# The last four bias steps placed inside the first two attention steps

## The chip, the cores and the metric

The kernel runs on one core of a Trainium2 chip. The metric is the device time of one execution in microseconds; lower is better. The core's engines take their own instructions in order: PE (matrix products), DVE, ACT and POOL (elementwise work), and SP, which here only issues DMA. "bias write" below is the ACT instruction that reads a bias step's product from PSUM.

## The reference

Attention with a learned relative-position bias, then a dense two-layer block on the attention output:

```python
scores = scale * np.matmul(q, k.transpose(0, 1, 3, 2))       # B 4, H 8, S 576, D 64
psi_rel = np.log1p(np.abs(rel))                              # rel = i - j
psi_i = np.log1p(np.maximum(pos[:, None], 1.0))
x = (psi_rel / psi_i)[..., None]
h = np.maximum(x @ w1 + b1, 0.0)                             # 32 hidden units
bias = h @ w2                                                # one value per head
scores = scores + bias.transpose(2, 0, 1)[None]
attn = np.exp(scores - max); attn = attn / (sum + 1e-09)
x = (attn @ v) as (2304, 512)
h = x @ w_in; r = np.maximum(h, 0.0); g = s * (r * r) + b    # w_in 512 x 2048
return g @ w_out
```

A constant added to one row of scores leaves the result as it is, since the row is normalised.

## The kernel before, in words

**Bias stage.** The 576 query rows are made in 36 steps of 16 rows (`STEPS`). A step has four *features* of 128 x 576 elements (4 query rows x 32 hidden units on the partitions), one for each `c` in 0 to 3. `feature` (L114 to L126) puts each on an engine by a letter: `v` is DVE (L121), `p` is POOL (L123), `a` is ACT (L125). The letters are "vvpa", "vppa", "vpvp" for steps 0, 1, 2 modulo 3; the last four steps have letters of their own (`ends`, L112). The features come from a pool of 16 buffers. `bias_step` (L131 to L154) multiplies the four features with the second layer's weights on PE (L140, L143) into a PSUM tile of two banks, writes the tile to SBUF on ACT (L147, tile `stg`), and lets SP store it to DRAM (L153, `bias`). From step 24 on `first_head` (L156 to L165) also copies head 0's rows straight into the tiles that the first pair reads: `bt` for rows below 512 (two DMAs a step), `be` for the last 64 rows (steps 32 to 35, two DMAs each). The stores of the last four steps are kept back until step 35.

PSUM has three pools here: `ps_s` (two tiles of two banks, scores), `ps_x` (one tile of two banks, the attention output) and `ps_t` (two banks, turns). Steps 2 modulo 3 use `ps_x`, the others `ps_s`.

**Attention stage.** There are 16 pairs (a head, two batches) of five blocks of 128 query rows: 80 blocks. `step(n)` (L525 to L561) runs in a software pipeline: `probs_t(n)` turns block n's exponentials on PE (L299) and copies them to the tile `pt` (ACT L330, DVE L332); `scores(n + 2)` makes the products on PE (L236) into `ps_s`; `biased` adds the bias on DVE (L250); `expo` takes the exponential on ACT (L261); and, from pair 1 on, `av` (L366, L369) makes the output of the pair before. In step 1 `probs_t` also takes the `ps_x` tile for a spare turn (L310). `split_qk` (L207 to L213) splits q or k of a pair into a high and a low part with two POOL instructions (L211, L212); scores need both. `load_w` fetches raw weight blocks and `fill` decodes them in pieces within the steps from pair 1 on, beginning with an ACT instruction (L407).

**Order.** The order is written out by hand: within each engine the instructions follow the order of the program. The loop at L599 makes the features of step `st + 2`, then runs step `st`, then what `plan` (L586 to L598) lists for `st`. So `scores(0)` stands behind step 33, `scores(1)` behind step 35, and `step(0)` behind the loop.

**Matrix stage.** From 286 us on, the two dense layers run (`expand`, L476; `project`, L501), with sums in 18 tiles `acc` of 128 x 512 in a pool of their own (L650).

Of the kernel before, what the change touches and what calls it, by code (L numbers as in the profile page):

```python
# [9 lines left out]
F32 = mybir.dt.float32  # L10
# [16 lines left out]
def attention_moe(ctx, tc, q, k, v, w_in, w_out, dist, par, out):  # L27
    nc = tc.nc
    NB, H, S, D = 2 * q.shape[0], q.shape[1], k.shape[3] - 64, q.shape[2] // 2
    DM, DFF = w_out.shape[1], w_out.shape[0]  # L30
    NT = out.shape[0]
# [4 lines left out]
    STEPS = S // 16  # L36
# [5 lines left out]
    LAST = 5 * NP  # L42
# [12 lines left out]
    ps_t = ps_ctx.enter_context(tc.tile_pool(name="ps_t", bufs=2, space=PSUM))  # L55
    pss_ctx = ExitStack()
    ps_s = pss_ctx.enter_context(tc.tile_pool(name="ps_s", bufs=2, space=PSUM, side="right"))
    dctx = ExitStack()
    dp = dctx.enter_context(tc.tile_pool(name="dp", bufs=1, side="right"))
    fp = dctx.enter_context(tc.tile_pool(name="fp", bufs=16, side="right"))  # L60
# [48 lines left out]
        nc.vector.tensor_copy(sb, pt_[:, 2:4])  # L109

    feats, late = {}, []
    ends = {STEPS - 4: "vvvp", STEPS - 3: "vvva", STEPS - 2: "vpva", STEPS - 1: "vpva"}  # L112

    def feature(st, c):  # L114
        w = NU - S - 16 * st - 4 * c
        f = fp.tile([128, S // 64, 68], F32, tag="f", name="f")[:, :, 0:64]
        src = ls[:, w:w + S].rearrange("p (a b) -> p a b", b=64)
        col = slice(4 * st + c, 4 * st + c + 1)
        kind = (ends.get(st) or ("vvpa", "vppa", "vpvp")[st % 3])[c]
        if kind == "v":  # L120
            nc.vector.tensor_scalar(f, src, thr[:, col], None, op0=ALU.max)  # L121
        elif kind == "p":
            nc.gpsimd.tensor_scalar(f, src, FLT_MAX, thr[:, col], op0=ALU.min, op1=ALU.max)  # L123
        else:
            nc.scalar.activation(f, src, AF.Relu, bias=off[:, col])  # L125
        return f, kind == "a"  # L126

    def bias_features(st):
        feats[st] = [feature(st, c) for c in (2, 0, 3, 1)]

    def bias_step(st):  # L131
        f2, f0, f3, f1 = feats.pop(st)
        fs = (f0, f1, f2, f3)
        if st % 3 == 2:
            ps = ps_x.tile([128, 2, 512], F32, tag="x", name="bps")
        else:
            ps = ps_s.tile([128, 2, 512], F32, tag="s", name="bps")
        pb = ps.rearrange("p a b -> p (a b)")
        for c in range(4):
            nc.tensor.matmul(  # L140
                pb[32 * c:32 * c + 32, 0:512], w2bd, fs[c][0][:, 0:8], start=True, stop=True)
        for c in range(4):
            nc.tensor.matmul(  # L143
                pb[32 * c:32 * c + 32, 512:S], w2bd, fs[c][0][:, 8:9], start=True, stop=True)
        kcol = kc[:, 1:2] if fs[3][1] else kc[:, 0:1]
        stg = fp.tile([128, S], F32, tag="stg", name="stg", bufs=10)
        nc.scalar.activation(stg, pb[:, 0:S], AF.Identity, scale=nr[:, st:st + 1], bias=kcol)  # L147
        if st >= 24:
            first_head(st, stg)
        late.append((st, stg))  # L150
        if st < STEPS - 4 or st == STEPS - 1:
            for i, t in late:
                nc.sync.dma_start(out=bias_d[:, 16 * i:16 * i + 16, :].rearrange("h r j -> r h j"), in_=t)  # L153
            late.clear()  # L154
# [16 lines left out]


    qs, ks, vals, tts, bts, pts, units, accs = {}, {}, {}, {}, {}, {}, {}, {}
    sums, rows, rts, rbs, bes, xts = {}, {}, {}, {}, {}, {}

    def load_bias(p, t0, t1):
        h = pairs[p][0]
# [111 lines left out]
    def probs_t(n):  # L289
        p, t = divmod(n, 5)  # L290
        if p not in pts:
            pts[p] = (ptp.tile([128, 4, 2, S], F32, tag="pt", name="pt"),
                      ptp.tile([128, S], F32, tag="ptr", name="ptr"))
        pt, ptr = pts[p]
        halves = [slice(64 * r, 64 * r + 64) for r in range(2)]

        def turn(outs, src, start=True):
            for r, d in enumerate(halves):
                nc.tensor.matmul(outs[r], src[d], ident[d, d], is_transpose=True,  # L299
                                 start=start, stop=True, skip_group_check=not start)  # L300

        def tail_of(t):
            return units[5 * p + t][0].rearrange("p x j -> p (x j)")[:, 512:640]

        def spare(j):
            c = HALF + 64 * j
            return [accs[p - 1][:, r, c:c + 64] for r in range(2)]

        if p == 0 and t == 1:
            accs[-1] = ps_x.tile([128, 2, 512], F32, tag="x", name="xps")  # L310
        if t == 3:
            nc.scalar.activation(
                ptr[:, 0:384].rearrange("p (t r c) -> p t r c", t=3, r=2),
                accs[p - 1][:, :, HALF:HALF + 192].rearrange("p r (t c) -> p t r c", t=3), AF.Copy)
        if (n + 1, 1) in tts:
            expo(n + 1, 1)
        pr = units[n][0]
        pss = [ps_t.tile([128, 512], F32, tag="t", name="tps") for _ in range(2)]
        if t < 4:
            for i in range(8):  # L320
                kb, x = divmod(i, 2)
                k0 = 64 * x + 128 * kb
                turn([ps[:, 64 * i:64 * i + 64] for ps in pss], pr[:, x, k0:k0 + 128])
            for j in ((), (0, 1), (2,), ())[t]:
                turn(spare(j), tail_of(j), start=(p == 0))
            for r, d in enumerate(halves):
                o = pt[:, :, :, 128 * t + 64 * r:128 * t + 64 * r + 64]
                i = pss[r].rearrange("p (a x b) -> p a x b", a=4, x=2)
                if r == 0:
                    nc.scalar.activation(o, i, AF.Copy)  # L330
                else:
                    nc.vector.tensor_copy(o, i)  # L332
            return
        for i in range(4):
            turn([ps[:, 64 * i:64 * i + 64] for ps in pss], pr[:, 0, 128 * i:128 * i + 128])
        turn([ps[:, 384:448] for ps in pss], tail_of(3))
        turn([ps[0:64, 256:320] for ps in pss], pr[:, 0, 512:S])
        turn([ps[0:9, 320:384] for ps in pss], rows.pop(p))
        rts[p] = sm.tile([9, 128], F32, tag="rt", name="rt", bufs=1)
        for r, d in enumerate(halves):  # L340
            for o, i in ((rts[p][:, d], pss[r][0:9, 320:384]),
                         (pt[:, :, r, 512:S], pss[r][:, 0:256].rearrange("p (a b) -> p a b", a=4)),
                         (ptr[d, 512:S], pss[r][0:64, 256:320]),
                         (ptr[:, 384 + 64 * r:448 + 64 * r], pss[r][:, 384:448])):
                if r == 0:
                    nc.scalar.activation(o, i, AF.Copy)
                else:
                    nc.vector.tensor_copy(o, i)
# [176 lines left out]
    def step(n):  # L525
# [3 lines left out]
        if cur:  # L529
            probs_t(n)  # L530
# [32 lines left out]
    early = [(kind, 0, i) for kind in range(2) for i in range(4)]  # L563
# [11 lines left out]
    def fill():  # L575
# [12 lines left out]
        11: ((load_bias, 0, 0, 1),),  # L588
        17: ((load_bias, 0, 1, 2),),
        20: ((load_v, 0), (load_be, 0)),  # L590
        28: ((split_qk, 0, 0),),
        30: ((split_qk, 0, 1),),
        26: ((load_bias, 0, 2, 3),),
        33: ((scores, 0), (biased, 0, 0), (expo, 0, 0), (biased, 0, 1)),
        35: ((expo, 0, 1), (scores, 1), (biased, 1, 0),
             (expo, 1, 0), (biased, 1, 1), (load_w, *early[0]), (load_w, *early[1]),
             (load_q, 2), (load_k, 2), (load_v, 1)),
    }  # L598
    for st in range(STEPS):  # L599
        if st + 2 < STEPS:  # L600
            bias_features(st + 2)
        bias_step(st)
        for fn, *args in plan.get(st, ()):
            fn(*args)
    dctx.close()
    ctx.enter_context(tc.tile_pool(name="pad2", bufs=1, side="right")).tile([128, 40], F32, name="pad2")
    wg0 = ctx.enter_context(tc.tile_pool(name="wg0", bufs=1, side="right", reuse_waits="tile"))
    alloc_w(0, wg0)
    wf = ctx.enter_context(tc.tile_pool(name="wf", bufs=1, side="right", reuse_waits="tile"))
    pctx = ExitStack()  # L610
    ptp = pctx.enter_context(tc.tile_pool(name="ptp", bufs=2, side="right", reuse_waits="tile"))
    decoding = {}

    def late_start(e):
# [5 lines left out]
        for _ in decoding.pop(e):  # L620
            pass

    for n in range(LAST - 2):
        step(n)
        if n == LAST - 10:
            for _ in filler:
                pass
            for a in range(KB - 1):
                load_x(0, a)
        if n == LAST - 4:  # L630
            load_x(0, KB - 1)
# [15 lines left out]
    pctx.close()  # L647
    ps_ctx.close()
    op = ctx.enter_context(tc.tile_pool(name="op", bufs=1, reuse_waits="tile"))
    acc = [op.tile([128, DM], F32, name=f"acc{k}") for k in range(NT // 128)]  # L650
    ps_o = ctx.enter_context(tc.tile_pool(name="ps_o", bufs=1, space=PSUM, reuse_waits="tile"))

    for a in range(KB):
# [104 lines left out]
```

## Time and profile before

| | us |
|---|---|
| median of 3 runs | 686.18 |
| the three runs | 686.15, 686.18, 689.35 |
| the profiled execution | 689.37 |
| its span, first to last instruction | 687.5 |
| PE busy | 665.2 (97%) |
| DVE busy | 456.4 (66%) |
| ACT busy | 353.6 (51%) |
| POOL busy | 181.5 (26%) |

The span is the time from the first to the last instruction of the profiled execution; the time of a run holds it and a little around it. Busy shares are means over the whole span, in which the bias stage (to about 52 us) and the first attention steps (to about 80 us) are a small part; they say little about those stages. In the rows, a stretch lists PE, PE's weight loads, DVE, ACT and POOL, then PE's granted clock, the DMA share and GB/s; in a timeline, `L123` is a line of the kernel, `out<-in` are its tiles, `xN` is the number of instructions merged in one row, and a bracket at the end tells how long the engine stood idle before the row and what ended that.

### The profile page before, as it was taken

To read this page: it belongs to the slowest core of one execution; us is meant where nothing else is said; L and a number is where in the kernel's file an instruction comes from. 1 tells how busy PE (TensorE), PEld (TensorE's weight loads), DVE (VectorE), ACT (ScalarE), POOL (GpSimd) and SP (SyncE) were. 2 spreads that over 40 slices of the span, in tenths; PEclk is the share of its full clock that TensorE was granted. 3 is DMA by queue.
4 is the path that set the end of the run, shared out by engine and by line. 5 is a ranking of instruction groups with operands and counts; after the bars stand their busy time and mean duration, and the time that the engine had idled before them with its cause. 6 is when DMAs were issued, how large, how long until landed. Compare 5 with 4: busy or idle time off the path is not lost.

```text
span 687.5 us, 13641 instructions
## 1 busy us (share of the span) xinstructions
PE 665.2 (97%) x5202; PEld 508.2 (74%) x5202; DVE 456.4 (66%) x883; ACT 353.6 (51%) x741; POOL 181.5 (26%) x190
## 2 busy tenths in 40 slices
PE   8987999999999999999999999999999999999997
PEld 4435667667676667578888888888888888888886
DVE  7996889988898888556576346665446655343344
ACT  6997767777677777534544333332333332322221
POOL 7992362345523450002222012121012220000000
PEclk9999999999999999999999999999999999999999
DMA  5976865656646734378745643216345204333312
GB/s 162 300 233 173 301 206 174 210 190 188 201 147 200 228 114 145 98 235 295 245 153 177 251 153 137 103 37 245 122 154 189 87 35 150 127 119 122 123 61 92
DMA packets 53872, 114.84 MB, mean 167 GB/s; under 512 B 10800, under 2 KB 18224, under 8 KB 53808
## 3 DMA queue, kind: packets, MB, share of 16 engines
q1 hardware_dynamic: 53664, 113.65, 49.8%
q8 instruction: 41, 0.67, 0.4%
q10 hardware_dynamic: 144, 0.33, 0.1%
q14 instruction: 23, 0.19, 0.1%
HBM read 83.77 MB, written 29.56 MB: 165 GB/s over the span
## 4 chain that ended last, share of the span: by engine, by line
PE 85%; DVE 4%; DMA 3%; POOL 3%; ACT 2%; issue 1%; SPq 1%; DVEq 0%; ACTq 0%; POOLq 0%
PE hps L476 29%; PE o L501 28%; PE sps L236 8%; PE xps L366 8%; PE tps L299 5%; PE bps L140 3%; PE xps L369 2%; DMA bias<-stg 2%; DVE tt L250 1%; POOL kr L212 1%; DMA qt<-in_q_dram 1%; POOL wl L429 1%; ACT stg L147 1%; POOL kr L211 1%; DMA pt__123<-in_par_dram 1%
## 5 line engine op out<-in xcount | busy, mean ns | idle before, releaser
L501 PE MATMUL o<-wh,gt 128*128 128x512 f32 x576 | 190.2, 389 | 0.0
L476 PE MATMUL hps<-x,wh 128*128 128x512 f32 (+1 forms) x640 | 181.8, 368 | 0.0
L480 ACT ACTIVATE r<-hps 128x512 f32<-128x512 f32 (+1 forms) x80 | 44.5, 556 | 212.8 <-PE hps L476 212.8
L481 DVE SCALAR_TENSOR_TENSOR r<-r,sb 128x512 f32<-128x512 f32 (+1 forms) x80 | 55.9, 698 | 143.9 <-ACT r L480 143.8
L261 ACT ACTIVATE pr<-tt,mn 128x576 f32<-128x576 f32 x144 | 110.9, 771 | 58.8 <-DVE mn L250 58.4
L476 PEld LDWEIGHTS hps<-x,wh 128*128 128x128 f32 x640 | 116.9, 188 | 22.1 <-ACT x L456 0.4
L501 PEld LDWEIGHTS o<-wh,gt 128*128 128x128 f32 x576 | 108.2, 188 | 22.3
L476 PE MATMUL hps<-x,wl 128*128 128x512 f32 (+1 forms) x320 | 117.7, 368 | 0.0
L501 PE MATMUL o<-wl,gt 128*128 128x512 f32 x288 | 112.2, 390 | 0.0
L429 POOL TENSOR_TENSOR wl<-full,wh 128x512 fp32r<-128x512 f32 x32 | 43.9, 1371 | 213.4 <-ACT wh L428 137.7
L250 DVE CUSTOM_DVE_ANT_0 tt<-sps,bt 128x576 f32<-128x576 f32 x128 | 91.3, 750 | 13.2 <-PE sps L236 12.9
L236 PE MATMUL sps<-kr,qr 64*128 64x288 f32 (+1 forms) x864 | 90.4, 310 | 7.7 <-POOL kr L212 5.1
L486 DVE SCALAR_TENSOR_TENSOR gt<-r,sb,gt 128x512 fp32r<-128x512 f32 (+1 forms) x80 | 62.7, 783 | 38.3 <-ACT gt L485 38.3
L236 PEld LDWEIGHTS sps<-kr,qr 64*128 64x128 f32 (+1 forms) x864 | 70.3, 186 | 12.3 <-POOL kr L212 6.1
L366 PE MATMUL xps<-pt,vt 128*64 128x288 f32 x512 | 77.0, 423 | 1.4 <-DVE rb L374 0.9
L485 ACT ACTIVATE gt<-r,sb 128x512 fp32r<-128x512 f32 (+1 forms) x80 | 54.4, 680 | 45.6 <-DVE r L481 45.5
L299 PEld LDWEIGHTS tps<-ident,pr 64*128 64x128 f32 x1216 | 44.7, 138 | 38.0 <-issue 27.5
L476 PEld LDWEIGHTS hps<-x,wl 128*128 128x128 f32 x320 | 60.3, 188 | 9.9
L501 PEld LDWEIGHTS o<-wl,gt 128*128 128x128 f32 x288 | 54.1, 188 | 10.5
L299 PE MATMUL tps<-ident,pr 64*128 64x64 f32 x1216 | 56.9, 230 | 4.0 <-ACT pt L330 2.0
L409 POOL TENSOR_SCALAR full<-full 128x512 f32<-128x512 f32 x32 | 23.9, 746 | 130.5 <-ACT full L407 130.1
L332 DVE COPY pt<-tps 128x512 f32<-128x512 f32 x64 | 44.0, 687 | 13.1 <-PE tps L299 13.0
(66 smaller groups left out, 704.8 us busy)
## 6 DMA issues: line engine op xcount, KB each, us to landing
x<-xs SPq DMA_DIRECT2D x48, 512.0 KB
bias<-stg SPq DMA_DIRECT2D x36, 288.0 KB
raw<-in_moe_w_in_dram SPq DMA_DIRECT2D x16, 512.0 KB
raw<-in_moe_w_out_dram SPq DMA_DIRECT2D x16, 512.0 KB
xs<-x SPq DMA_DIRECT2D x16, 512.0 KB
bt<-bias SPq DMA_DIRECT2D x7, 1152.0 KB
qt<-in_q_dram SPq DMA_DIRECT2D x16, 320.0 KB
kt<-in_k_dram SPq DMA_DIRECT2D x16, 320.0 KB
```

The lines of the kernel that those rows point to most:

```text
L236: nc.tensor.matmul(o, a, b, start=(i == 0), stop=(i == 2))
L250: nc.vector.tensor_tensor_reduce(tt.rearrange("p (a b) -> p a b", a=2), ps[x][:, :, 0:HALF], bias.rearrange("p (a b) -> p a b", a=2), -1.0 ...
L261: nc.scalar.activation(pr[:, x], tts.pop((n, x)), AF.Exp, bias=mn[:, x:x + 1], scale=-1.0, accum_out=sums[p][:, col:col + 1])
L299: nc.tensor.matmul(outs[r], src[d], ident[d, d], is_transpose=True, start=start, stop=True, skip_group_check=not start)
L366: nc.tensor.matmul(ps[64 * x:64 * x + 64, hf, 0:HALF], vt[:, 4 * x + kb, :], pt[:, kb, x, c], start=(kb == 0), stop=False)
L429: nc.gpsimd.tensor_tensor(lo, full, hi.bitcast(F32), op=ALU.subtract)
L476: nc.tensor.matmul(ps[:, 0:n], w[0, g][:, a, fc], xs_t[s, a][:, j, 0:n], start=(i == 0), stop=(i == 3 * KB - 1))
L480: nc.scalar.activation(r, ps[:, 0:n], AF.Relu)
L481: nc.vector.scalar_tensor_tensor(r, r, sb[:, 0:1], r, op0=ALU.mult, op1=ALU.mult)
L485: nc.scalar.activation(hi, r, AF.Identity, bias=sb[:, 1:2])
L486: nc.vector.scalar_tensor_tensor(lo, r, sb[:, 1:2], hi.bitcast(F32), op0=ALU.add, op1=ALU.subtract)
L501: nc.tensor.matmul(o, gt[:, a, tok], w[1, g][:, fo], start=(fo == 0 and j == 0), stop=(fo == 3 and j == 2))
```

## The change

Steps 32 to 35 move into attention. Their features are no longer made two steps ahead but from the plan: step 32's and 33's behind the work of blocks 0 and 1, 34's behind `step(0)`, 35's behind step 33. `scores(0)` moves from step 33 to step 30, `scores(1)` from step 35 to step 31, `step(0)` to step 32 and `step(1)` behind step 35. The letters of the last four steps are all "vpap": one DVE, two POOL, one ACT (before, together, ten DVE, three POOL, three ACT). Steps 30 to 35 all use the `ps_x` tile. The stores of six steps, 30 to 35, are kept back. The splits of pair 0 move from steps 28 and 30 to 23 and 25; the loads of q and k of pair 2 and v of pair 1 move from step 35 to step 28, and the first two raw weight blocks stand behind `step(1)`, which itself reloads the bias for head 1. Pair 0's `pt` can no longer wait for the bias stage's buffers to be given up, so even pairs have a pool of their own, `ptp0`; its tile later holds the first nine sums `acc`.

```diff
+    ctx.enter_context(tc.tile_pool(name="pad2", bufs=1, side="right")).tile([128, 40], F32, name="pad2")
+    ptp0 = ctx.enter_context(tc.tile_pool(name="ptp0", bufs=1, side="right"))
...
-    ends = {STEPS - 4: "vvvp", STEPS - 3: "vvva", STEPS - 2: "vpva", STEPS - 1: "vpva"}
-
...
-        kind = (ends.get(st) or ("vvpa", "vppa", "vpvp")[st % 3])[c]
+        kind = ("vpap" if st >= STEPS - 4 else ("vvpa", "vppa", "vpvp")[st % 3])[c]
...
-        if st % 3 == 2:
+        if st % 3 == 2 or st >= STEPS - 6:
             ps = ps_x.tile([128, 2, 512], F32, tag="x", name="bps")
...
-        if st < STEPS - 4 or st == STEPS - 1:
+        if st < STEPS - 6 or st == STEPS - 1:
...
-            pts[p] = (ptp.tile([128, 4, 2, S], F32, tag="pt", name="pt"),
-                      ptp.tile([128, S], F32, tag="ptr", name="ptr"))
+            pool = ptps[p % 2]
+            pts[p] = (pool.tile([128, 4, 2, S], F32, tag="pt", name="pt"),
+                      pool.tile([128, S], F32, tag="ptr", name="ptr"))
...
-        28: ((split_qk, 0, 0),),
-        30: ((split_qk, 0, 1),),
+        23: ((split_qk, 0, 0),),
+        25: ((split_qk, 0, 1),),
         26: ((load_bias, 0, 2, 3),),
-        33: ((scores, 0), (biased, 0, 0), (expo, 0, 0), (biased, 0, 1)),
-        35: ((expo, 0, 1), (scores, 1), (biased, 1, 0),
-             (expo, 1, 0), (biased, 1, 1), (load_w, *early[0]), (load_w, *early[1]),
-             (load_q, 2), (load_k, 2), (load_v, 1)),
+        28: ((load_q, 2), (load_k, 2), (load_v, 1)),
+        30: ((scores, 0), (biased, 0, 0), (biased, 0, 1), (expo, 0, 0), (bias_features, 32)),
+        31: ((expo, 0, 1), (scores, 1), (biased, 1, 0), (biased, 1, 1), (expo, 1, 0),
+             (bias_features, 33)),
+        32: ((step, 0), (bias_features, 34)),
+        33: ((bias_features, 35),),
+        35: ((step, 1), (load_w, *early[0]), (load_w, *early[1])),
     }
     for st in range(STEPS):
-        if st + 2 < STEPS:
+        if st + 2 < STEPS - 4:
             bias_features(st + 2)
...
-    ptp = pctx.enter_context(tc.tile_pool(name="ptp", bufs=2, side="right", reuse_waits="tile"))
+    ptps.append(pctx.enter_context(tc.tile_pool(name="ptp1", bufs=1, side="right", reuse_waits="tile")))
...
-    for n in range(LAST - 2):
+    for n in range(2, LAST - 2):
...
-    acc = [op.tile([128, DM], F32, name=f"acc{k}") for k in range(NT // 128)]
+    first = ptp0.tile([128, 9, DM], F32, tag="pt", name="acc")
+    acc = [first[:, k] for k in range(9)]
+    acc += [op.tile([128, DM], F32, name=f"acc{k}") for k in range(9, NT // 128)]
```

## Rows read from the trace of the kernel before

**Rows 1.** Chain that ended last; a stretch's busy us and instructions by engine, clock, DMA.

```profile
PE 85%; DVE 4%; DMA 3%; POOL 3%; ACT 2%; issue 1%; SPq 1%; DVEq 0%; ACTq 0%; POOLq 0%
...
30.00:40.00 10.00, 9.67 (x143) 4.68 (x133) 10.00 (x15) 10.00 (x15) 10.00 (x15) 1.00 0.92 281
```

**Rows 2.** Timeline of POOL: start us, us, engine, line, operation, tiles, count.

```profile
5.51 36.81 POOL L123 TENSOR_SCALAR f<-ls,thr 128x576 f32<-128x576 f32 x51 [4.21 <-DVE ls L100]
42.41 0.73 POOL L211 TENSOR_SCALAR qr<-qt 128x640 fp32r<-128x640 f32 x1
...
44.88 2.18 POOL L123 TENSOR_SCALAR f<-ls,thr 128x576 f32<-128x576 f32 x3
```

**Rows 3.** Timeline of DVE: its features, and the first bias add (b0).

```profile
7.64 44.01 DVE L121 TENSOR_SCALAR f<-ls,thr 128x576 f32<-128x576 f32 x61
52.32 0.76 DVE L250 CUSTOM_DVE_ANT_0 tt<-sps,bt 128x576 f32<-128x576 f32 x1 [0.68 <-PE sps L236]
```

**Rows 4.** Timeline of ACT, 42 to 59 us: bias writes, features, exponentials, P copy.

```profile
42.88 0.82 ACT L147 ACTIVATE stg<-bps,kc,pt__123 128x576 f32<-128x576 f32 x1
43.60 0.77 ACT L125 ACTIVATE f<-ls,off 128x576 f32<-128x576 f32 x1
44.26 1.65 ACT L147 ACTIVATE stg<-bps,kc,pt__123 128x576 f32<-128x576 f32 x2
...
47.70 0.83 ACT L147 ACTIVATE stg<-bps,kc,pt__123 128x576 f32<-128x576 f32 x1 [1.12 <-issue]
...
50.48 0.82 ACT L147 ACTIVATE stg<-bps,kc,pt__123 128x576 f32<-128x576 f32 x1
53.12 0.78 ACT L261 ACTIVATE pr<-tt,mn 128x576 f32<-128x576 f32 x1 [1.83 <-DVE mn L250]
...
57.89 0.76 ACT L261 ACTIVATE pr<-tt,mn 128x576 f32<-128x576 f32 x1
...
58.65 0.57 ACT L330 ACTIVATE pt<-tps 128x512 f32<-128x512 f32 x1
```

**Rows 5.** Timeline of PE: bias step 31, scores(0), scores(10), with their waits.

```profile
46.39 0.63 PE L140 MATMUL bps<-f,pt__123 128*32 128x512 f32 x3 [0.78 <-POOL f L123]
...
51.35 1.05 PE L236 MATMUL sps<-kr,qr 64*128 64x288 f32 x11 [1.03 <-ACT stg L147]
...
79.99 0.92 PE L236 MATMUL sps<-kr,qr 64*128 64x288 f32 x10 [1.11 <-POOL kr L212]
```

**Rows 6.** Timeline of SP's DMA issues: last rows, stores kept back, raw weight blocks.

```profile
57.62 4.98 SPq L165 DMA_DIRECT2D be<-stg  x8
62.64 2.53 SPq L153 DMA_DIRECT2D bias<-stg  x4
65.21 2.46 SPq L395 DMA_DIRECT2D raw<-in_moe_w_in_dram  x2
```

**Rows 7.** Timeline of DVE: first bias adds of blocks 3, 4 and 10.

```profile
61.46 0.76 DVE L250 CUSTOM_DVE_ANT_0 tt<-sps,bt 128x576 f32<-128x576 f32 x1 [0.52 <-PE sps L236]
...
64.38 0.76 DVE L250 CUSTOM_DVE_ANT_0 tt<-sps,be 128x576 f32<-128x576 f32 x1 [0.88 <-ACT pt L330]
...
80.95 0.76 DVE L250 CUSTOM_DVE_ANT_0 tt<-sps,bt 128x576 f32<-128x576 f32 x1 [0.73 <-PE sps L236]
```

**Rows 8.** Timeline: ACT reads the first raw block; POOL begins pair 2's split.

```profile
72.99 0.65 ACT L407 ACTIVATE full<-raw 128x512 f32<-128x512 f32 x1
...
74.38 0.73 POOL L211 TENSOR_SCALAR qr<-qt 128x640 fp32r<-128x640 f32 x1 [18.54 <-DMA qt<-in_q_dram]
```

**Rows 9.** Busy us and granted clock by stretch; one output product group, twice.

```profile
95.00:96.00 1.00, 0.18 (x2) 0.18 (x4) 0.97 (x2) 0.68 (x2) 0.92 (x2) 1.00 0.90 276
...
97.00:98.00 1.00, 1.00 (x6) 0.51 (x8) 0.99 (x3) 0.13 (x1) 0.92 (x2) 0.50 1.00 349
...
80.84 1.19 PE L366 MATMUL xps<-pt,vt 128*64 128x288 f32 x8
...
96.91 2.19 PE L366 MATMUL xps<-pt,vt 128*64 128x288 f32 x8
```

More of the change, by code (lines that the diff above doesn't have):

```diff
@@ L173, in attention_moe @@
     qs, ks, vals, tts, bts, pts, units, accs = {}, {}, {}, {}, {}, {}, {}, {}
-    sums, rows, rts, rbs, bes, xts = {}, {}, {}, {}, {}, {}
+    sums, rows, rts, rbs, bes, xts, ptps = {}, {}, {}, {}, {}, {}, [ptp0]
     def load_bias(p, t0, t1):
@@ L605, in attention_moe @@
     dctx.close()
-    ctx.enter_context(tc.tile_pool(name="pad2", bufs=1, side="right")).tile([128, 40], F32, name="pad2")
     wg0 = ctx.enter_context(tc.tile_pool(name="wg0", bufs=1, side="right", reuse_waits="tile"))
```

## Prediction

> **What bounds the kernel now.** I read the chain of waits first. Most of the span is a chain on PE [rows 1], so what happens early is worth the time by which it moves the start of that chain, and no more. The change touches only the first 80 us, so I read the engines there. Until about 45 us three engines are full together: in the stretch from 30 to 40 DVE, ACT and POOL are busy for all 10 us [rows 1]. POOL makes 51 features without a gap, 0.722 us each [rows 2], DVE 61 at 0.721 us [rows 3]: three bias steps, of five DVE, five POOL and two ACT features and three bias writes, take 3.6 us. There is no free engine in the bias stage, and POOL is the one to watch: step 0 of attention cannot begin without the split of q and k, which is POOL's too. Split q takes 2.47 us of POOL's queue, from 42.41 to the next feature at 44.88 [rows 2].
>
> From 52 us to 70 us the kernel walks through attention steps 0 to 4. Nothing is full there; each step waits for a ring of scores on PE, bias add on DVE, exponential on ACT and turn on PE. I follow it by the first bias add of each scores block, b0 at 52.32 [rows 3], b3 (issued in step 1) at 61.46, b4 (step 2) at 64.38 and b10 (step 8) at 80.95 [rows 7]. Two waits there come from late DMA: DVE stands 0.88 us before b4 [rows 7], whose rows SP issued last, until 62.60 [rows 6]; and PE stands 1.11 us in front of scores(10) [rows 5], since POOL got q of pair 2 only at 74.38 [rows 8]. From b10 on PE leads.
>
> **The splits move ahead.** Both splits of pair 0 go from behind features 30 and 32 to behind 25 and 27. At the old place three POOL features are left between the two splits [rows 2], and the full stretch ends there. The size of a split's delay when it bites: the bias write of step 31 would be due three steps, 3.60 us, after that of step 28 at 42.88, at 46.48, and came at 47.70, 1.22 us late [rows 4], PE having waited for POOL until 46.39 [rows 5]. So of 2.47 us POOL had a lead of 1.25. At the new place two splits, 4.94 us, fall in the full stretch: steps 28 to 31 come 4.94 - 1.25 = 3.7 us late. POOL ended feature 30 at 42.32 (5.51 + 36.81) and the last of step 29 one feature earlier, at 41.60; now at 46.54.
>
> **One bank in place of three.** Steps 29 to 35 now all use the output's PSUM tile, which has one buffer. A step's matmuls start, its ACT write begins 1.31 us later (46.39 to 47.70), lasts 0.83, and the next step's matmuls follow at once (51.35 against 50.48 + 0.82) [rows 4, 5]: 2.2 us a step. Step 29: matmuls 46.6, write 47.9 to 48.7. Step 30: matmuls 48.8. Behind them on PE scores(0) at about 50.0 (some 1.2 us of matmuls, an estimate from the 1.31), in place of 51.35 [rows 5]. What the deferral promised, scores(0) ahead of three bias steps, is worth 1.35 us at this point. b0 is 0.97 us behind (51.35 to 52.32), its exponential 0.80 behind that (52.32 to 53.12) [rows 3 to 5]: 51.77.
>
> **The ACT run.** ACT takes its work in the order of the program. From the first exponential it now meets: exp, feature 32, write 31, exp, exp, feature 33, write 32, exp, P copy, exp, feature 34, then write 33. Its start-to-start times are 0.72 for a write (42.88 to 43.60), 0.66 for a feature (43.60 to 44.26), 0.76 for an exponential (57.89 to 58.65) and 0.57 for the copy [rows 4]: five exponentials 3.80, three features 1.98, two writes 1.44, the copy 0.57, sum 7.8 us. I find no point in it where ACT would wait: POOL's features for 32 and 33 are done by 50.2 and 51.6 (0.722 each behind 48.7). Write 33 goes from 59.6 to 60.4. Now the bank loop sets the pace, for nothing else is left between: matmuls 34 at 60.45, write 61.8 to 62.6, matmuls 35 at 62.65, write 64.0 to 64.8. POOL, with two more features each and pair 1's q split ahead of feature 34, has 35 done at 57.0 (51.6 + 2.47 + 4 x 0.722), in time.
>
> **Step 1 is queued behind steps 34 and 35 on PE.** It also writes its spare turn in that same PSUM tile. Behind write 35, scores(3) starts at about 65.1 and b3 at 66.1; before, 61.46 [rows 7]. That is **4.6 us late**. Six DVE features fewer cost nothing and give nothing: DVE is not last here.
>
> **What is given back.** The rows of steps 32 to 35 are no longer behind a full SP queue: two issues of 0.62 us behind write 35 end at 66.1 and land 1.8 us later (64.38 against 62.60) [rows 6, 7], 67.9. b4 without its wait would follow b3 by 64.38 - 0.88 - 61.46 = 2.04, at 68.1: 3.7 us late. Pair 2's q and k and pair 1's v are issued at step 28, some 17 us earlier than before; that takes three issues on SP ahead of the rows of step 29, where SP is not behind by then because the bias writes come late. The 1.11 us in front of scores(10) goes: 2.6 us late.
>
> **A load that comes later.** The first two raw weight blocks were issued at 65.21 and ACT reads the first at 72.99 without a wait [rows 6, 8], so one takes at most 7.8 us to land, and at least the 1.8 of a small store. Now SP has, behind the two row issues, six deferred stores at 0.63 us [rows 6], then the reload of the bias for head 1 (two issues, about 1.2 us, an estimate from those), then the raw blocks: 66.1 + 3.8 + 1.2 = 71.1. They land between 73 and 79. ACT wants the first at 72.99 + 3.7 = 76.7, so it stands 0 to 2.2 us, and behind it are the exponential and P copies of the next step. I take the middle, 1.1.
>
> **Sum.** 4.6 - 0.9 - 1.1 + 1.1 = 3.7 us. The profiled execution took 689.37 us, span 687.5, and would become 693.1; it is one of the slower ones, for two of the three timed runs are at 686.2. Against the median, 686.18 + 3.7 = **689.9**. The first nine accumulators in the even pairs' P tile, the pools and the address shifts I cost at nothing: that tile is last read in the output product of pair 14, hidden behind the last steps' PE work, and its first new writer comes after a whole token block.
>
> **Rivals.** (1) The raw blocks land in time: 2.6 us late, 688.8. For it: the 7.8 us is only an upper bound.
> (2) POOL's delay doesn't arrive, because it has more lead than the 1.25 us read off one event. Then everything from step 28 on is up to 3.7 us earlier: b3 0.9 late, b4 level, and the wait before scores(10) gained: 685.1. Against it: PE's wait for POOL at 46.39 is plain.
> (3) The overlap works in full, not slower but faster: the four steps are 16 features and 4 writes, 20 pieces of 0.72 us on three engines, 4.8 us, all inside attention's idle time, with the two waits (0.88 and 1.11) gone: 6.8 us, 679.4. It decides at scores(3): it needs them before 59, which needs writes 33 to 35 not to be in one row behind one bank.
> (4) The clock. PE was busy 0.18 us in the stretch 95 to 96, and the granted clock fell to 0.50 (the 1.2 GHz level) by 97 to 98, where a group of eight matmuls took 2.19 us, against 1.19 us for the same group earlier at 2.4 GHz [rows 9]. My schedule leaves PE idle for about 2 us before matmuls 34 and 1 us before 35. A fall there doubles the turns, scores and two bias steps around it; at a price of the 1.0 us seen for one group and half of that for the next, 1.5 us: 691.4. Against it: PE's wait of 1.11 us up to 79.99 brought no fall, since the group at 80.84 took its 1.19 us [rows 5, 9]. The Trainium skill, TensorE: Matmul & The Clock Gate, section What's actually happening, says that the low clock is the default and comes back after idleness; the trace agrees at 96 us.
> (5) The engines' order is not the program's, and the steps run as before: about 688. Before, the order on ACT and PE follows the program throughout.
>
> **How the numbers follow.** Half a per cent, 3.43 us, is about what a measurement of this kernel can tell from no change: slower means over 689.6. The forecast has 0.42, and 688.3 to 691.5 as its own range; it lies on the edge, so 0.28 of it is slower and 0.14 the same. The clock 0.13 (slower). Rivals 1 and 2, 0.14 each, and 5, 0.03: the same. Rival 3, 0.14: faster. Faster 0.14, same 0.45, slower 0.41. The range leaves out most of rival 3 and the far end of 4 with the raw blocks at their latest: 684.0 to 693.0.
>
> **What would show it.** In the changed kernel: PE waiting for POOL's features in steps 26 to 29, the write of step 29 near 47.9; scores(0) near 50; writes 33, 34 and 35 on ACT 2.2 us apart, with ACT and PE both idle between; b3 near 66; no wait on POOL before scores(10); ACT idle in front of its first read of a raw block. If b3 comes before 61.5, the forecast's first half is wrong; if b10 comes before 81, its sign is.

## The result and the profile after

| | before | after |
|---|---|---|
| median | 686.16 us (6 runs, 684.72 to 689.36) | 696.65 us (6 runs, 694.7 to 698.78) |
| ratio | | 1.0137, 95% interval 1.0116 to 1.0159 |
| the profiled execution: time, span | 689.37, 687.5 | 694.7, 692.7 |
| mean granted clock of PE in it | 0.997 | 0.993 |

The change makes the kernel 10.5 us slower by the medians, and 9.4 us (8.0 to 10.9) by the ratio. The two profiled executions differ by only 5.3 us: that of before is the slowest of its six, that of after the fastest. So I read from the traces where the time goes, and take how much from the timed runs.

ACT after, its timeline: the bias writes of steps 29, 33, 34 and 35, the first exponential, and the first read of a raw block. The columns are start us, us, engine, line, and in brackets the idle time ahead of the row with what ended it.

```profile
47.58 0.83 ACT L147 ACTIVATE stg<-bps,kc,pt__130 128x576 f32<-128x576 f32 x1
...
51.47 0.78 ACT L261 ACTIVATE pr<-tt,mn 128x576 f32<-128x576 f32 x1 [0.84 <-DVE mn L250]
...
59.19 0.82 ACT L147 ACTIVATE stg<-bps,kc,pt__130 128x576 f32<-128x576 f32 x1
...
61.36 0.83 ACT L147 ACTIVATE stg<-bps,kc,pt__130 128x576 f32<-128x576 f32 x1 [0.68 <-ACT f L125]
64.51 0.83 ACT L147 ACTIVATE stg<-bps,kc,pt__130 128x576 f32<-128x576 f32 x1 [2.32 <-PE bps L143]
...
81.95 0.66 ACT L408 ACTIVATE full<-raw 128x512 f32<-128x512 f32 x1 [3.10 <-DMA raw<-in_moe_w_in_dram]
```

PE after, its timeline: bias step 28 behind POOL, step 30 behind the bank, scores(0), steps 34 and 35 behind the bank, the turns of step 1, turns behind ACT's stand, and scores(10):

```profile
44.84 0.63 PE L140 MATMUL bps<-f,pt__130 128*32 128x512 f32 x3 [2.56 <-POOL f L123]
...
48.47 1.06 PE L140 MATMUL bps<-f,pt__130 128*32 128x512 f32 x8 [1.02 <-ACT stg L147]
...
49.58 1.05 PE L236 MATMUL sps<-kr,qr 64*128 64x288 f32 x12
...
60.06 1.07 PE L140 MATMUL bps<-f,pt__130 128*32 128x512 f32 x8 [2.21 <-ACT stg L147]
...
62.24 1.94 PE L140 MATMUL bps<-f,pt__130 128*32 128x512 f32 x8 [1.00 <-ACT stg L147]
...
64.32 1.11 PE L300 MATMUL tps<-ident,pr 64*128 64x64 f32 x16
...
83.91 0.71 PE L300 MATMUL tps<-ident,pr 64*128 64x64 f32 x15 [2.70 <-ACT pt L331]
...
88.75 1.03 PE L236 MATMUL sps<-kr,qr 64*128 64x288 f32 x12
```

DVE after, the first bias adds of blocks 0, 3, 4, 8, 9 and 10:

```profile
50.66 0.76 DVE L250 CUSTOM_DVE_ANT_0 tt<-sps,bt 128x576 f32<-128x576 f32 x1 [6.61 <-PE sps L236]
...
67.55 0.76 DVE L250 CUSTOM_DVE_ANT_0 tt<-sps,bt 128x576 f32<-128x576 f32 x1 [1.35 <-PE sps L236]
...
69.56 0.76 DVE L250 CUSTOM_DVE_ANT_0 tt<-sps,be 128x576 f32<-128x576 f32 x1
...
80.03 0.76 DVE L250 CUSTOM_DVE_ANT_0 tt<-sps,bt 128x576 f32<-128x576 f32 x1 [0.35 <-PE sps L236]
...
86.08 0.76 DVE L250 CUSTOM_DVE_ANT_0 tt<-sps,be 128x576 f32<-128x576 f32 x1 [0.73 <-PE sps L236]
...
89.94 0.75 DVE L250 CUSTOM_DVE_ANT_0 tt<-sps,bt 128x576 f32<-128x576 f32 x1
```

The adds of blocks 8 and 9 before:

```profile
74.27 0.76 DVE L250 CUSTOM_DVE_ANT_0 tt<-sps,bt 128x576 f32<-128x576 f32 x1 [0.36 <-PE sps L236]
...
77.08 0.76 DVE L250 CUSTOM_DVE_ANT_0 tt<-sps,be 128x576 f32<-128x576 f32 x1 [0.44 <-PE sps L236]
```

b0 comes 1.7 us earlier than before [rows 3], b3 6.1 later, b4 5.2 later, b10 9.0 later [rows 7]. Of these 9.0 us only 5.3 are left at the end, for the trace of before loses time on the way too: it has its own fall of the clock at 96 to 100 us [rows 9], and takes 155.9 us from b20 to b75 (the first bias adds of blocks 20 and 75), where that of after takes 153.8. From b75 to the end both take 419.8 us.

Three things stand in these rows. PE waits for the one bank, 2.21 and 1.00 us. From 62 us on it works at half the clock: the eight matmuls of a bias step take 1.94 us and not 1.07, the turns 1.11 and not 0.71. And ACT stands 3.10 us for the first raw block. The granted clock by stretch (PE, PE's weight loads, DVE, ACT, POOL, clock, DMA share, GB/s):

```profile
62.00:68.00 6.00, 5.76 (x64) 4.12 (x66) 1.14 (x2) 2.26 (x5) 0.00 (x0) 0.50 0.14 40
...
85.00:89.00 4.00, 4.00 (x34) 2.37 (x34) 1.45 (x4) 2.23 (x7) 0.76 (x1) 0.57 0.88 257
```

Both falls stand behind a stretch in which PE waited: the first behind the 2.21 us for the bank up to 60.06 (the matmuls that follow still take 1.07 us, those at 62.24 take 1.94), the second behind the 2.70 us for ACT up to 83.91.

The chain that ended last, of the kernel after, in order of time, shows why the raw block is late (start us, us, what):

```profile
64.51 0.84 ACT stg L147
...
65.36 0.49 SPq L165
...
65.90 0.59 SPq L165
...
66.53 0.59 SPq L153
...
70.80 0.91 SPq L182
...
71.76 0.79 SPq L183
...
72.59 9.34 DMA raw<-in_moe_w_in_dram
```

The first raw block is issued 8.1 us behind the write of step 35, because SP issues that step's rows, six deferred stores and the reload of the bias first; it then lands 9.34 us later. Between 72 and 82 us the DMA engines are busy 0.88 of the time; that the block waits behind the bytes of the stores and the reload is read from this order, no run tests the bytes alone. What SP does is released by step 35, so a block that ACT must read before it can go on hangs on the last bias step.

### The profile page after: what moved, and what is told of

It is laid out like the page before. It is cut to its first block, busy times and chain, and to the rows that moved or that the text cites. A ratio compares the mean times of both kernels' runs of the same rounds, so it can differ in the third digit from the quotient of the medians.

```text
span 692.7 us, 13634 instructions
## 1 busy us (share of the span) xinstructions
PE 667.6 (96%) x5202; PEld 511.1 (74%) x5202; DVE 447.9 (65%) x877; ACT 353.5 (51%) x742; POOL 185.3 (27%) x195
## 4 chain that ended last, share of the span: by engine, by line
PE 81%; DVE 2%; DMA 2%; POOL 2%; SPq 2%; ACT 1%; issue 1%; DVEq 0%; ACTq 0%; POOLq 0%
PE hps L477 29%; PE o L502 28%; PE sps L236 8%; PE xps L367 8%; PE tps L300 5%; PE xps L370 2%; DMA raw<-in_moe_w_in_dram 1%; DVE tt L250 1%; POOL kr L212 1%; DMA kt<-in_k_dram 1%; SPq L153 1%; POOL wl L430 1%; POOL kr L211 0%; ACT stg L147 0%; SPq L199 0%
```

## Experiments: the three delays, one at a time

The four kernels of this section ran on one chip beside the kernel before, whose median there was 687.54 us, against 686.16 beside the changed kernel. So each gain is given twice: by the medians, against 696.65, and by the ratios to the kernel before, against 1.0137 (1.0116 to 1.0159).

**The raw blocks earlier.**

```diff
-        32: ((step, 0), (bias_features, 34)),
+        32: ((load_w, *early[0]), (load_w, *early[1]), (step, 0), (bias_features, 34)),
...
-        35: ((step, 1), (load_w, *early[0]), (load_w, *early[1])),
+        35: ((step, 1),),
```

> The changed kernel with one edit: the first two raw weight blocks are issued by SP ahead of step 0, not behind step 1. Theory S (a sum of separate delays: steps 33 to 35 in one bank ahead of step 1 on PE, the clock at half rate twice, the raw block 3.1 us late on ACT): ACT's wait of 3.10 us in front of its first read of a raw block goes, PE's wait of 2.70 us at 83.9 with it, and the clock does not fall at 86 us; b10 comes 3 to 4 us earlier than the 89.94 of the changed kernel, b3 stays within 0.5 us of 67.55, and the time falls by 3 to 4.5 us. Rival C (the clock alone carries what is over the forecast, the raw block's wait is hidden behind it): under 1 us. Rival P (the new pools and the sums in the P tile cost time in the later stages): 0.

692.40 us, ratio to before 1.0078 (1.0047 to 1.0109), 4.3 us under the changed kernel (4.0 by the ratios, whose intervals do not overlap). ACT reads the block with no wait, at 79.95:

```profile
79.86 0.19 ACT L261 ACTIVATION_READ_ACCUMULATOR pr<-tt,mn 128x1 f32 x1
79.95 0.66 ACT L408 ACTIVATE full<-raw 128x512 f32<-128x512 f32 x1
```

From b8 to b9 it takes 2.8 us, as before, and not 6.1. b3 is at 68.17, 0.62 us later and not within 0.5, and b10 at 87.67, 2.3 us earlier and not 3 to 4. The clock still fell, by 46, 63 and 77 us, so that part of what was expected did not come: the falls need no raw block. The late block is a delay of its own, of 3 to 4 us.

**Step 34 out of the bank.**

```diff
-        if st % 3 == 2 or st >= STEPS - 6:
+        if st % 3 == 2 or (st >= STEPS - 6 and st != STEPS - 2):
```

> The changed kernel with one edit: step 34 uses the scores' PSUM tiles again, so that steps 33, 34 and 35 are no longer in one row behind one bank. Theory S: the matmuls of step 34 start at about 59.3 and not at 60.06, those of step 35 at about 60.8 and not 62.24, b3 comes at 64 to 64.5 if the clock still falls and earlier if it doesn't, against 67.55; the time falls by 2 to 3.5 us. Rival Q (ACT's run of exponentials, features and writes, not the bank, holds step 1): under 0.7 us. Rival P: 0.

692.51 us, ratio 1.0080 (1.0051 to 1.0110), 4.1 us under the changed kernel (3.9 by the ratios, clear of noise too). ACT's writes of steps 33, 34, 35 in this kernel:

```profile
60.88 0.82 ACT L147 ACTIVATE stg<-bps,kc,pt__130 128x576 f32<-128x576 f32 x1
62.30 0.83 ACT L147 ACTIVATE stg<-bps,kc,pt__130 128x576 f32<-128x576 f32 x1
63.69 0.83 ACT L147 ACTIVATE stg<-bps,kc,pt__130 128x576 f32<-128x576 f32 x1 [0.56 <-DMA be<-stg]
...
80.45 0.66 ACT L408 ACTIVATE full<-raw 128x512 f32<-128x512 f32 x1 [3.25 <-DMA raw<-in_moe_w_in_dram]
```

They are 1.4 us apart, not 2.2 and 3.2. b0 to b3 takes 13.5 us (52.36 to 65.89) and not 16.9 (50.66 to 67.55), of which the clock has a part. It is the bank that holds step 1, not ACT's order. But b3 misses the 64 to 64.5 expected, since b0 itself is 1.7 us later than in the changed kernel's trace: the clock fell here at 45 us, behind PE's wait for POOL's features (the stretch with the columns of above):

```profile
45.32 1.05 PE L140 MATMUL bps<-f,pt__130 128*32 128x512 f32 x3 [2.57 <-POOL f L123]
...
46.00:48.00 2.00, 2.00 (x19) 0.62 (x14) 0.00 (x0) 0.45 (x1) 2.00 (x3) 0.50 0.65 175
```

The last row of ACT's says something that I had not expected: ACT stands 3.25 us for the raw block here too, although everything is earlier. The block follows the write of step 35 (16.8 us here, 17.4 in the changed kernel), so a shorter bias stage brings the need and the block forward together, and the bank's cure leaves the late block as it is.

**Three POOL features on DVE.**

```diff
+        if st in (26, 28, 29) and c == 1:
+            kind = "v"
```

> The changed kernel with one edit: one POOL feature each of steps 26, 28 and 29 goes to DVE, which stood idle for 6.6 us before b0. Theory S (POOL's two splits make steps 26 to 31 late, and everything behind them): step 29's write comes 1.5 to 2.2 us earlier than 47.58, and so do b0 (50.66) and b3 (67.55); the time falls by 1.5 to 2.2 us. Rival Q (the run on ACT and the bank loop take up the difference): b0 earlier, b3 by under 0.7 us. Rival P: 0.

695.63 us, ratio 1.0113 (1.0068 to 1.0159). b0 is 1.2 us earlier:

```profile
49.49 0.76 DVE L252 CUSTOM_DVE_ANT_0 tt<-sps,bt 128x576 f32<-128x576 f32 x1 [3.01 <-PE sps L238]
```

and b3, at 66.62, is 0.9 earlier, less than the 1.5 to 2.2 expected. POOL's delay is passed on to step 1, but it is the smallest of the three; the time, 1.0 us less (1.6 by the ratios), cannot tell it from nothing.

**PE kept busy while it waits.**

```diff
+    def keep_busy(k):
+        ps = ps_t.tile([128, 512], F32, tag="t", name="dps")
+        for _ in range(k):
+            nc.tensor.matmul(ps, ident, ls[:, 0:512], start=True, stop=True)
...
         bias_step(st)
+        if st in (STEPS - 3, STEPS - 2):
+            keep_busy(2 if st == STEPS - 3 else 1)
```

> The changed kernel with work added: two matmuls of 512 columns behind bias step 33 and one behind step 34, into a turn tile that nobody reads, so that PE is busy while it would wait for the bank. They add under 2 us to PE where it stood idle for 2.2 and 1.0 us. Theory S: the clock stays at 1.00 from 60 to 70, the turns behind step 35 take 0.71 us and not 1.11, b3 comes at 66.0 to 66.5 against 67.55, the time falls by 1 to 2 us. Rival C (the clock carries more than that): 4 us or more. If the clock falls at the same place all the same, idleness of PE there is not what lowers it, and the time is the same or up to 0.5 us longer.

Median 692.06 us, ratio 1.0103 (1.0061 to 1.0146): by the medians 4.6 us faster than the changed kernel, by the ratios 2.3, and the two intervals overlap. The five executions lie in two groups, 691.7 to 692.1 at mean clocks of 0.997 to 0.999 and 695.2 to 698.1 at 0.990 to 0.993, so the median says little, and whether the time falls by theory S's 1 to 2 us or by rival C's 4 isn't shown. The added matmuls took 3.1 us of PE (1.98 and 1.12), not under 2. In the profiled one the stretch from 58 to 66 us keeps its clock; two stretches of this kernel, with the columns of above:

```profile
58.00:62.00 4.00, 3.46 (x26) 1.25 (x28) 2.91 (x7) 4.00 (x9) 1.58 (x2) 1.00 0.18 57
62.00:66.00 4.00, 3.73 (x50) 1.55 (x42) 0.21 (x1) 1.97 (x4) 0.00 (x0) 1.00 0.12 37
```

and the same two of the changed kernel:

```profile
58.00:62.00 4.00, 1.18 (x16) 0.42 (x16) 1.45 (x3) 3.32 (x6) 1.12 (x1) 0.91 0.15 43
62.00:66.00 4.00, 3.76 (x38) 2.14 (x40) 0.49 (x1) 1.68 (x5) 0.00 (x0) 0.50 0.09 28
```

In these two executions PE was busy for 3.46 of the first 4 us and kept the clock, or for 1.18 and worked at half of it right behind. b0 to b3 takes 15.1 us here:

```profile
52.33 0.76 DVE L250 CUSTOM_DVE_ANT_0 tt<-sps,bt 128x576 f32<-128x576 f32 x1 [7.79 <-PE sps L236]
...
67.41 0.76 DVE L250 CUSTOM_DVE_ANT_0 tt<-sps,bt 128x576 f32<-128x576 f32 x1 [0.92 <-PE sps L236]
```

In the changed kernel it takes 16.9, so this fall costs 1.8 us, and without it the changed kernel would have b3 at 50.66 + 15.1 = 65.7 (an estimate from the two traces). The idle time of PE in front of steps 34 and 35 costs twice, once as itself and once as a clock. The profiled execution as a whole, 695.24 us, is no faster than that of the changed kernel: the clock fell in it by 46 us, behind POOL, and by 83, behind the raw block.

The traces of the other edited versions of the changed kernel, one execution each, bear this out. Behind the waits for the bank the clock fell, between 59 and 63 us, in all four that have them and no added matmuls (the changed kernel, the raw blocks earlier, the features on DVE, and the old letters, below). In this one, and in the three with step 34 in the scores' tiles (above, and two below, one of them with other added matmuls), it did not fall there. Behind the raw block, for which ACT stands 3.0 to 3.6 us, it fell in all five that have that wait. And behind PE's wait of 2.5 to 2.6 us for POOL it fell, by 46 us, in four of five; where three features are on DVE that wait is 0.4 to 0.5 us and the clock stayed. In those four b0 is at 52.1 to 52.4 and not at 50.66, against 52.32 before: the lead that scores(0) gained by its earlier place is gone.

## Experiments: what they leave, and the rest of the change

The next four ran on a second chip, where the kernel before had a median of 686.85.

**The three edits together** (raw blocks, bank, POOL features).

> The changed kernel with three edits together: the raw weight blocks ahead of step 0, step 34 in the scores' tiles, one POOL feature each of steps 26, 28 and 29 on DVE. Theory S (separate delays that add): from b0 near 49.5 to b3 13.5 us, b3 at about 63.0 where the clock does not fall; no wait of ACT for a raw block; b10 near 80.5 against 80.95 of the kernel before; 7 to 10 us under the changed kernel, 686 to 689.5, what is left over the kernel before being falls of the clock. Rival P (the new pools, or the sums in the P tile, cost time that none of these edits touches): 690 or more.

686.51 us, ratio 1.0019 (0.9987 to 1.0050). By the medians they gave 4.3, 4.1 and 1.0 singly, 9.4 in sum, and together 10.1 of the 10.5 us; by the ratios 4.0, 3.9 and 1.6, and together 8.1 of 9.4. The three delays, with the clock that follows on them, are the whole loss, as far as this interval can tell (0.9 us faster to 3.4 slower than the kernel before). b3 is at 62.97 as expected. But b10 was at 88.48 and not near 80.5 in the profiled execution, one of the slowest of its twelve, for DVE stood in front of b4:

```profile
69.66 0.76 DVE L252 CUSTOM_DVE_ANT_0 tt<-sps,be 128x576 f32<-128x576 f32 x1 [4.64 <-DMA be<-stg]
```

With the raw blocks moved ahead, the rows of step 35 follow a megabyte in the DMA queue, and in this execution landed late; the clock fell for 14 us behind it. The cure for one late load made another late. The other executions are 684.5 to 690.5 and one at 693.7.

**The old letters.**

```diff
+    ends = {STEPS - 4: "vvvp", STEPS - 3: "vvva", STEPS - 2: "vpva", STEPS - 1: "vpva"}
...
-        kind = ("vpap" if st >= STEPS - 4 else ("vvpa", "vppa", "vpvp")[st % 3])[c]
+        kind = (ends.get(st) or ("vvpa", "vppa", "vpvp")[st % 3])[c]
```

> The changed kernel with the old letters for the last four steps: ten DVE, three POOL and three ACT features instead of four, eight and four. Theory S (POOL has the features of steps 32 to 35 ready long before their matmuls, which wait for the bank): no gain, b3 within 0.7 us of 67.55 apart from the clock, and up to 1 us longer, since three DVE features then stand ahead of block 1's bias add. Rival G (half of the features on POOL is what costs): 2 to 4 us faster.

699.54 us, ratio 1.0176 (1.0138 to 1.0215): 2.9 us slower still by the medians, though with four executions the interval overlaps that of the changed kernel. DVE makes three features between the adds of blocks 0 and 1:

```profile
52.08 0.76 DVE L252 CUSTOM_DVE_ANT_0 tt<-sps,bt 128x576 f32<-128x576 f32 x1 [7.84 <-PE sps L238]
...
53.44 2.25 DVE L123 TENSOR_SCALAR f<-ls,thr 128x576 f32<-128x576 f32 x3
55.61 0.75 DVE L252 CUSTOM_DVE_ANT_0 tt<-sps,bt 128x576 f32<-128x576 f32 x1
```

b0 to b1 takes 3.5 us and not 2.5, and b0 to b3 18.5 and not 16.9; b3, at 70.54, is 3.0 us later than in the changed kernel, where at most 1 was expected apart from the clock. Half of the features on POOL is not what costs, and rival G falls: in this place it helps, by 1.6 us in the trace, and I had priced it at nothing.

**The memory part alone**, in the kernel before:

```diff
+    ptp0 = ctx.enter_context(tc.tile_pool(name="ptp0", bufs=1, side="right"))
...
+            pool = ptps[p % 2]
+            pts[p] = (pool.tile([128, 4, 2, S], F32, tag="pt", name="pt"),
+                      pool.tile([128, S], F32, tag="ptr", name="ptr"))
...
+    first = ptp0.tile([128, 9, DM], F32, tag="pt", name="acc")
+    acc = [first[:, k] for k in range(9)]
...
```

> The kernel before with the memory part of the change alone: P of the even pairs in a pool of its own, nine of the sums in its tile. Theory S: the same time as before, within 0.5 us. Rival P: 1 to 4 us slower, to be seen from 286 us on, where the sums are written.

687.35 us, ratio 1.0003 (0.9978 to 1.0028): no difference, as forecast, though the interval alone leaves room for the lower end of rival P (up to 1.9 us slower). The traces settle it where rival P looked, in the matrix stage: from b75 to the end this kernel takes 419.8 us (265.08 to 684.88), as the kernel before (267.72 to 687.47) and the changed one (272.92 to 692.75) do. Rival P falls.

**Pair 2's loads ahead of the raw blocks**, in the kernel before:

```diff
-             (expo, 1, 0), (biased, 1, 1), (load_w, *early[0]), (load_w, *early[1]),
-             (load_q, 2), (load_k, 2), (load_v, 1)),
+             (expo, 1, 0), (biased, 1, 1), (load_q, 2), (load_k, 2),
+             (load_w, *early[0]), (load_w, *early[1]), (load_v, 1)),
```

> The kernel before with q and k of pair 2 issued ahead of the first two raw weight blocks and not behind them. Theory S (PE's wait of 1.11 us before scores(10) comes from that load's place in SP's queue): q lands 2 us earlier, the wait goes, b10 at 79.8 against 80.95; ACT still reads its raw block without a wait; 0.5 to 1.2 us faster. Rival H (the wait comes from the weight decode ahead of the split in POOL's queue): the same time.

685.98 us, ratio 0.9997 (0.9974 to 1.0020). PE's wait before scores(10) is not in the trace, and POOL's split of q begins at 71.73 and not 74.38 [rows 8]. But b10 came at 83.54, since the clock fell from 66 to 76 us in that execution. One wait of 1.1 us is less than what the clock does from run to run; whether it is a gain stays open.

**The bank alone**, in the kernel before, on a third chip (before there: 686.35):

```diff
-        if st % 3 == 2:
+        if st % 3 == 2 or st >= STEPS - 6:
```

> The kernel before with one part of the change alone: steps 30 to 35 all use the output's PSUM tile. Theory S (2.2 us a step once they share one bank): from step 31 on each step's matmuls wait for the write before; scores(0) stands behind step 33, so b0 comes 1.5 to 2 us later than 52.32, b3 about 2.2 us later than 61.46, the time rises by 1.5 to 2.5 us. Rival Q (ACT's order, not the bank, paces these steps): under 0.5 us.

688.68 us, ratio 1.0037 (1.0020 to 1.0054), 2.3 us more. The writes of steps 30, 31 and 32, whose matmuls have no POOL delay and no exponentials between:

```profile
46.49 0.83 ACT L147 ACTIVATE stg<-bps,kc,pt__123 128x576 f32<-128x576 f32 x1 [1.40 <-issue]
48.72 0.83 ACT L147 ACTIVATE stg<-bps,kc,pt__123 128x576 f32<-128x576 f32 x1 [0.73 <-ACT f L125]
50.90 0.83 ACT L147 ACTIVATE stg<-bps,kc,pt__123 128x576 f32<-128x576 f32 x1 [0.68 <-ACT f L125]
```

2.2 us apart, where three banks gave 1.4 at this place [rows 4]. b3 is 3.9 us later in the profiled execution, 1.7 more than expected, and the clock fell at 52 to 55 us in it, again behind waits of PE for the bank.

**Added work for PE, once more.** One matmul of 192 columns in each of steps 1 to 4 and two ahead of scores(15), into columns that nobody reads: alone in the kernel before, with the three edits in the changed kernel, and with pair 2's loads in the kernel before.

```diff
             scores(m)
+            if 1 <= n <= 4:
+                nc.tensor.matmul(accs[-1][:, 0, 0:192], ident, ident_w, start=True, stop=True)
...
+        if n == 15:
+            nc.tensor.matmul(ps[0][:, 0, 0:192], ident, ident_w, start=True, stop=True)
+            nc.tensor.matmul(ps[0][:, 0, 0:192], ident, ident_w, start=True, stop=True)
```

> The kernel before with work added for PE alone: one matmul of 192 columns behind the scores in each of steps 1 to 4, two ahead of scores(15), into PSUM columns that nobody reads, where PE stood idle for 0.4 to 0.7 us a step and for 1.2 us before scores(15). Theory S (the falls of the clock between 60 and 100 us come from PE's idleness there and cost about 0.5 to 0.7 us for each thousandth of mean clock): the granted clock stays at 1.00 in more executions, the mean clock rises from 0.996 to 0.998 or more, 0.5 to 2 us faster than before. Rival N (the added matmuls only delay the next turn on PE): the same or up to 1 us slower.

> The changed kernel with the three edits (raw weight blocks ahead of step 0, step 34 in the scores' tiles, three POOL features on DVE) and the same added matmuls. Theory S: the falls between 60 and 100 us become rarer, the time goes from about 686.5 to 685 or so, with fewer executions above 688; against the kernel before the same to 2 us faster. If the change's plan held a gain that the three delays only covered, it would be 682 or less here. Rival N: 686.5 to 687.5.

> The kernel before with q and k of pair 2 ahead of the raw weight blocks and with the added PE work of steps 1 to 4 and ahead of scores(15). Theory S: b10 at about 80, fewer falls of the clock, 1 to 2 us faster than before, 685 to 686. Rival N: within 0.7 us of before.

In this order: 686.39 us, ratio 0.9991 (0.9973 to 1.0009); 686.38 us, 0.9991 (0.9968 to 1.0013); 685.33 us, 0.9987 (0.9966 to 1.0008). The kernel before had 686.89 beside the first two, 686.35 beside the third. The mean clock over the executions rises from 0.9961 in the kernel before (its 87 runs on four chips) to 0.9984, 0.9979 and 0.9982, which is the sign that theory S gave, but no ratio is clear of 1. A version that beats the kernel before isn't shown. The third's profiled execution, the slowest of its twelve, has b10 at 83.60 and not at about 80, behind a fall at 79 to 83 us. In the profiled executions of the first two the clock never fell; the change with its delays cured has these adds of blocks 3, 4 and 10:

```profile
62.83 0.76 DVE L258 CUSTOM_DVE_ANT_0 tt<-sps,bt 128x576 f32<-128x576 f32 x1 [0.90 <-PE sps L244]
...
65.68 0.76 DVE L258 CUSTOM_DVE_ANT_0 tt<-sps,be 128x576 f32<-128x576 f32 x1 [0.80 <-DMA be<-stg]
...
80.99 0.75 DVE L258 CUSTOM_DVE_ANT_0 tt<-sps,bt 128x576 f32<-128x576 f32 x1
```

The kernel before with the same added work, also at a full clock, has b10 here:

```profile
81.23 0.76 DVE L256 CUSTOM_DVE_ANT_0 tt<-sps,bt 128x576 f32<-128x576 f32 x1 [0.73 <-PE sps L242]
```

So even cured the plan is worth 0.2 us at that point, the spans are 683.8 and 683.3, and the medians on one chip are 686.38 and 686.39: a gain that the delays covered isn't seen.

## Why the prediction was wrong in size

It forecast slower by 3.7 us, with 684 to 693 as its range; 10.5 us came. The order of events was right and nearly to the time, and so was the sign, though the largest chance, 0.45, stood on no change that a measurement can tell. Two terms were mis-sized.

- **The splits move ahead: right.** PE waited for POOL's features (2.56 us in front of step 28), the write of step 29 came at 47.58 (forecast 47.9), scores(0) at 49.58 (50.0). What the forecast left out is that a fall of the clock can follow this wait of PE too: one did in four of five traces, and took back what scores(0) had gained.
- **One bank, 2.2 us a step: right**, shown by undoing it (4.1 us) and by doing it alone (2.3 us).
- **The ACT run: right.** Write 33 at 59.19 (59.6), write 34 at 61.36 (61.8), matmuls 35 at 62.24 (62.65).
- **b3 4.6 us late: right without the clock.** 65.7 by the execution that kept its clock there, against 66.1, so 4.2 late; in the trace 67.55.
- **What is given back: right.** b4 has no wait, scores(10) none for POOL's split. At b10 the second cannot be seen in this trace: from b9 it takes 3.86 us, as before (3.87), since the clock was at half in between. That SP would not be behind at step 29 was wrong, but cost nothing: it issued that step's rows at 53.09, though the write had ended at 48.41, and b3, which needs them, came later still.
- **The late raw block, 1.1 us: wrong.** It was 3.10 us on ACT, and b8 to b9 grew by 3.24 (6.05 against 2.81). The step that failed took "at most 7.8 us to land" from before, where the raw blocks were issued behind four stores, and of the wait of 0 to 2.2 us that follows it the middle. Behind six stores and 1.3 MB of reload the block took 9.34 us, and 8.0 to 9.0 in the four other traces that have it at this place: never within the bound. It was also issued at 72.59 and not at 71.1. A bound from one place of a queue doesn't hold at another: that it is the bytes ahead which lengthen it is argued.
- **The clock, a rival at 0.13 and 1.5 us: under-priced in both.** I counted one possible fall, and held against it one wait of 1.11 us that had brought none; the new waits of PE were 2.56, 2.21 and 2.70 us. Each is a place for a fall: in the profiled execution they came behind the bank and behind the raw block, and over the six runs the mean clock was 0.9897. What a fall costs can be read from the 87 runs of the kernel before: eleven at a mean clock of 0.9985 and more have a median of 684.64, the nineteen below 0.9945 (mean 0.9926) 688.45, so 0.52 us for each thousandth. The change lowers the mean by 6.4 thousandths (0.9961 to 0.9897): 3.3 us, an estimate from these runs (a straight line through all 87 gives 0.43 and 2.8).
- **The rest at nothing: right** for the memory part (1.0003). The letters were priced at nothing and save 1.6 us from b0 to b3 where they stand; the time, 696.65 against 699.54, agrees in sign but isn't clear of noise.

With the sizes measured the sum is 4.2 - 0.9 - 1.1 for step 1 and what is given back, 3.2 for the raw block, 3.3 for the clock: 8.7 us, of 10.5 by the medians and 9.4 (8.0 to 10.9) by the ratio. Whether anything is left isn't shown: the sum lies within that interval. That falls of the clock come from PE's waits is shown in front of step 34, where the added matmuls or a second tile kept them away, and the features on DVE kept them away at POOL's wait; that all of the lower mean comes from such waits is argued.

The bound of the range failed because it had the raw block at no more than 2.2 us and the clock at one fall of 1.5, where 3.2 and 3.3 came. The two are separate delays, as the range had them: with the raw blocks earlier the clock still fell behind the bank, and with step 34 out of the bank the block was still 3.25 us late. In the changed kernel's trace both came.

## What to carry to other kernels

When work is moved into idle time, look first at what stands behind it in each engine's queue: here step 1 stood behind three bias steps that shared one buffer, and a weight load behind the DMAs that the last of them releases. A load's landing time is not carried over from its old place: here at most 7.8 us became 8.0 to 9.3. And an added wait of PE is priced with a fall of the clock behind it, not as a rare misfortune: behind the waits that this change adds, a fall stood in nearly every trace.

## What the runs showed of the hardware that I had not expected

Work that computes nothing can keep a clock: with 3.1 us of added matmuls in an idle stretch PE held its full clock where it had fallen to half, and b0 to b3 took 15.1 us and not 16.9. That it saves time over the whole kernel (692.06 against 696.65) isn't clear of noise.

The same kernel before takes from 683.7 to 690.6 us in its 87 runs, and the mean granted clock goes along with about half of that (684.64 at 0.9999, 688.45 at 0.9926). The rest is something else: at one mean clock, 0.995, its runs still lie between 686.3 and 689.8. In the 14 traces no fall stands between 100 us and the last microsecond, yet the stretch from b20 to b75 takes 152.9 to 155.9 us; from b75 to the end all of them take 419.8 to 419.9. What makes the difference between b20 and b75 stays open.
